# Twenty of a head's 64 score chunks moved from VectorE to TensorE in a decode step with its backward pass

## The chip, the cores and the metric

One Trainium2 chip; the program runs on 1 core. The metric is device time in microseconds (us) of one execution. A profile is one execution, and its span is a few us shorter than the timed run. Ratios are not quite the ratios of the medians that stand beside them.

## The reference, cut to what matters

A decode step (one token, D = 640) with an attention block over a cache and an MLP block, followed by the gradients of nine inputs. The attention has 32 heads, each with its own K and V cache of 8192 x 192 in bf16, and almost all bytes and time go there:

```python
q = (x @ wq).reshape(B, Sq, Hq, Dh).transpose(0, 2, 1, 3)      # Sq = 1, Hq = 32, Dh = 192
scores = einsum('bhqd,bhkd->bhqk', q, k) * Dh ** (-0.5)
p = softmax(scores, axis=-1)
o = einsum('bhqk,bhkd->bhqd', p, v)
# ... o @ wo, gates, MLP block; then jax.vjp of the whole for grad_out
```

The kernel works in two parts. The forward reads K and V of each head once (6.3 MB), makes the scores, and keeps the exponentials E of all heads and a matrix M = sum over keys of E * k v^T, from which the backward gets what it needs of q's gradient without reading K again. The backward reads V again and writes dK and dV. The change concerns the forward only.

## The kernel before: the parts that matter

A head's 8192 keys lie on 128 partitions, 64 "chunks" of 192 values each per partition, loaded in two halves of 32 chunks (1.5 MB each). Scores of a half are made on VectorE: one product with q, three halvings, one sum.

```python
def load_k(h, t):                       # 5 K buffers
    kb = KB[(2 * h + t) % NKB]
    nc.sync.dma_start(out=kb, in_=K_hd[h][:, t * JH : (t + 1) * JH, :])
def load_v(h, t):                       # 3 V buffers, the same SyncE queue
    vb = VB[nv[0] % NVB]
    nc.sync.dma_start(out=vb[:, :, 2 : 2 + PW], in_=...)

def dot_half(src4, vec, dst):           # VectorE, 32 chunks
    V_.tensor_tensor(out=prod, in0=src4, in1=vec(broadcast), op=mult)
    w = DH
    for _ in range(3):
        w //= 2
        V_.tensor_tensor(out=prod[:, :, 0:w], in0=prod[:, :, 0:w], in1=prod[:, :, w:2*w], op=add)
    V_.reduce_sum(out=dst, in_=prod[:, :, 0:w])

def softmax(h, S_h):                    # max over the head: VectorE, TensorE, VectorE, then E on ScalarE
    V_.reduce_max(out=m1, in_=S_h)
    T_.matmul(mx, lhsT=m1(broadcast), rhs=ident_f)
    V_.reduce_max(out=negm, in_=mx, negate=True)
    A_.activation(out=E4, in_=S_h(x4), func=Exp, bias=negm)
    ...

def scale_k(q, kb, E4, Ef):             # a quarter: E * K, 10 chunks on VectorE, 6 on ScalarE, 3 buffers KS
    ...
def m_quarter(q, ks, vb, mp):           # TensorE, 32 matmuls a quarter: (E * K)^T V, frees the V buffer
    ...
for i in range(HQ + 1):                 # scores of head i beside scaling and value matmuls of head i - 1
    kh = [load_k(i, 0), load_k(i, 1)]; vh = [load_v(i, 0)]
    for t in range(2):
        dot_half(kh[t], q_of_head_i, S_h[half t])
        for q in (2 * t, 2 * t + 1):    # of head i - 1
            m_quarter(q, scale_k(q, ...), pv[t], mp)
        if t == 0: vh.append(load_v(i, 1))
    E4, Ef = softmax(i, S_h)
    m_out(i - 1, mp)                    # copies M out; small matmuls "po" for the output columns
    # every second head: load wo and the next wq, q_pair() for the next two heads, pair_out()
```

The source says what depends on what. The order of the instructions on each engine is not that of the source: it is fixed when the program is compiled, once for all, and each engine then works through its own list in that order (the traces of the changed kernel and of e16 below, two programs with the same lists, show 8659 TensorE, 1657 VectorE and 2529 ScalarE records in the same order).

Of the kernel before, what the change touches and what calls it, by code (L numbers as in the profile page):

```python
# [8 lines left out]
FP32 = mybir.dt.float32  # L9
BF16 = mybir.dt.bfloat16  # L10
# [10 lines left out]
def kernel(  # L21
# [27 lines left out]
    P = 128  # L49
    D = A_x.shape[-1]  # L50
    _, HQ, S, DH = A_k_cache.shape
# [3 lines left out]
    J = S // P  # L55
    JH = J // 2
    JQ = J // 4
    ND = D // P
# [7 lines left out]
    MW = DH + 4  # L66
# [4 lines left out]
    V_, A_, T_ = nc.vector, nc.scalar, nc.tensor  # L71

    const = ctx.enter_context(tc.tile_pool(name="const", bufs=1))
# [77 lines left out]
    def bcast_cols(src, n, out, eng):  # L151
        tp = psS.tile([NF, P], FP32, name="bc_t", tag="s")
        T_.transpose(out=tp[0:n, :], in_=src, identity=ident_f)
        rows = tmp.tile([NF, P], BF16, name="bc_rows")
        eng(out=rows[0:n, :], in_=tp[0:n, :])
        for g in range(0, n, 4):
            m = min(4, n - g)
            ps = psB.tile([P, 512], FP32, name="bc_ps", tag="b")
            for b in range(m):
                T_.matmul(ps[:, b * P : (b + 1) * P], lhsT=pick(n, g + b), rhs=rows[0:n, :], start=True, stop=True)  # L160
            eng(out=out[:, g * P : (g + m) * P], in_=ps[:, 0 : m * P])
# [104 lines left out]
        return vb  # L266

    def dot_half(src4, vec, dst):
        prod = pp.tile([P, JH, DH], BF16, name="prod", tag="prod")
        V_.tensor_tensor(  # L270
            out=prod.rearrange("p (a b) d -> p a b d", b=2),
            in0=src4,
            in1=vec[:, None, None, :].to_broadcast([P, JH // 2, 2, DH]),
            op=ALU.mult,
        )
        w = DH
        for _ in range(3):
            w //= 2
            V_.tensor_tensor(out=prod[:, :, 0:w], in0=prod[:, :, 0:w], in1=prod[:, :, w : 2 * w], op=ALU.add)  # L279
        V_.reduce_sum(out=dst, in_=prod[:, :, 0:w], axis=AX.X)  # L280

    NKB = 5
    NVA = (3 * JQ) // 8
    MO = 256
    last = {}
    with tc.tile_pool(name="kp", bufs=1) as kp, tc.tile_pool(name="ks", bufs=1) as ksp:
        KB = [None] * NKB
        for k in range(NKB):
            b = (2 * (HQ - 1) + 2 + k) % NKB
# [9 lines left out]
        def load_k(h, t):  # L299
            kb = KB[(2 * h + t) % NKB]  # L300
            nc.sync.dma_start(out=kb, in_=K_hd[h][:, t * JH : (t + 1) * JH, :])
            return kb

        def softmax(h, S_h):
            m1 = tcol(1, "m1")
            V_.reduce_max(out=m1, in_=S_h, axis=AX.X)
            mx = psX.tile([P, P], FP32, name="mx", tag="mx")
            T_.matmul(mx, lhsT=m1[:, 0:1].to_broadcast([P, P]), rhs=ident_f, start=True, stop=True)
            negm = tcol(1, "negm")
            V_.reduce_max(out=negm, in_=mx, axis=AX.X, negate=True)  # L310
            E4 = tmp.tile([P, J, 4], BF16, name="E4")
            A_.activation(out=E4, in_=S_h[:, :, None].to_broadcast([P, J, 4]), func=ACT.Exp, bias=negm[:, 0:1], scale=1.0)
            A_.copy(out=E_all[:, h, :], in_=E4[:, :, 0])
            Ef = tmp.tile([P, J], FP32, name="Ef")
            A_.copy(out=Ef, in_=E4[:, :, 0])
            return E4, Ef

# [28 lines left out]
        def m_out(h, mp):  # L346
            t = h // 2
            A_.copy(out=M1[:, h, :], in_=mp[:, 0:MW])  # L348
            orow = tmp.tile([P, MW], FP32, name="orow")
            A_.copy(out=orow[64:65, :], in_=mp[64:65, MO : MO + MW])  # L350
            ov = orow[64:65, 2 : 2 + DH]
            one = ones_f[64:65, :]
            if h % 2 == 0:
                A_.copy(out=M2[0:64, t, :], in_=mp[0:64, MO : MO + MW])
                po = psO.tile([P, 8], FP32, name="po")
                last["po"] = po
                cols = ((0, 0, P, 0), (1, 0, 64, P))
            else:
                V_.tensor_copy(out=M2[64:128, t, :], in_=mp[0:64, MO : MO + MW])
                po = last["po"]  # L360
                cols = ((1, 64, P, 0), (2, 0, P, 64))
            for b, lo, hi, d0 in cols:
                T_.matmul(po[lo:hi, b : b + 1], lhsT=ov[:, d0 : d0 + hi - lo], rhs=one[:, 0:1], start=True, stop=True)
                T_.matmul(po[lo:hi, 3 + b : 4 + b], lhsT=one[:, 0 : hi - lo], rhs=orow[64:65, 0:1], start=True, stop=False)
                T_.matmul(po[lo:hi, 3 + b : 4 + b], lhsT=one[:, 0 : hi - lo], rhs=orow[64:65, MW - 1 : MW], start=False, stop=True)

        def pair_out(t, wo_t):
            po = last["po"]
            rz = tcol(3, "rz")
            V_.reciprocal(out=rz, in_=po[:, 3:6])  # L370
            V_.tensor_tensor(out=o_col[:, 3 * t : 3 * t + 3], in0=po[:, 0:3], in1=rz, op=ALU.mult)
            V_.tensor_copy(out=rinv[:, 2 * t : 2 * t + 2], in_=rz[:, 0:3:2])
            o2 = tmp.tile([P, 3, 2], BF16, name="o2")
            V_.tensor_tensor(out=o2, in0=omask, in1=o_col[:, 3 * t : 3 * t + 3, None].to_broadcast([P, 3, 2]), op=ALU.mult)
            ps = psS.tile([P, ND, 2], FP32, name="ao_ps", tag="s")
            for i in range(ND):
                for k in range(3):
                    T_.matmul(ps[:, i, :], lhsT=wo_t[:, k, i * P : (i + 1) * P], rhs=o2[:, k, :], start=(k == 0), stop=(k == 2))
            A_.copy(out=AO[:, :, 2 * t : 2 * t + 2], in_=ps)
# [5 lines left out]
        for i in range(HQ + 1):  # L385
            if i < HQ:
                if i == 0:
                    q_pair(0, w_next)
                kh = [load_k(i, 0), load_k(i, 1)]
                vh = [load_v(i, 0)]  # L390
                S_h = tmp.tile([P, J], FP32, name="S_h")
            mp = psM.tile([P, 512], FP32, name="mp", tag="m") if i > 0 else None
            for t in range(2):
                if i < HQ:
                    dot_half(kh[t].rearrange("p (a b) d -> p a b d", b=2), qs_bc[:, i * DH : (i + 1) * DH], S_h[:, t * JH : (t + 1) * JH])
                if i > 0:
                    pk, pv, pE4, pEf = st[i - 1]
                    for q in (2 * t, 2 * t + 1):
                        ks = scale_k(q, pk[t], pE4, pEf)
                        m_quarter(q, ks, pv[t], mp)  # L400
                if i < HQ and t == 0:
                    vh.append(load_v(i, 1))
            if i < HQ:
                E4, Ef = softmax(i, S_h)
                st[i] = (kh, vh, E4, Ef)
            if i > 0:
                m_out(i - 1, mp)
                if (i - 1) % 2 == 0:
                    wo_t = load_wo((i - 1) // 2)
                    if i + 1 < HQ:  # L410
                        w_next = load_w(wq_v, ((i + 1) // 2) * PW)
                        q_pair((i + 1) // 2, w_next)
                else:
                    pair_out((i - 1) // 2, wo_t)
                    if g_next < NMB // 3 and i >= 2:
                        for _ in range(2):
                            if g_next < NMB // 3:
                                mod_chunk(g_next, load_w(wm_v, g_next * PW))
                                g_next += 1
                st.pop(i - 1)  # L420
# [8 lines left out]
    dx1 = col(ND, "dx1")  # L429
    dao = col(ND, "dao")  # L430
    dao_bf = col(ND, "dao_bf", BF16)
    dao_bc = const.tile([P, D], BF16, name="dao_bc")
    cpr = col(HQ, "cpr")
    ckS = col(NQ, "ckS")
    with tc.tile_pool(name="mid", bufs=1) as mid, tc.tile_pool(name="mst", bufs=2) as mst:
# [109 lines left out]
        for i in range(ND):  # L545
            o3 = mst.tile([P, F], BF16, name="o3")
            V_.tensor_scalar(out=o3, in0=du_bc, scalar1=n2[:, i : i + 1], scalar2=None, op0=ALU.mult)
            nc.gpsimd.dma_start(out=out_6[i * P : (i + 1) * P, :], in_=o3)
        bcast_cols(dao, ND, dao_bc, A_.copy)


    with tc.tile_pool(name="bk1", bufs=1) as bk1, tc.tile_pool(name="ob", bufs=4) as ob, tc.tile_pool(name="bst", bufs=2) as bst:
        do_bc = bk1.tile([P, QD], BF16, name="do_bc")
        dha = bk1.tile([P, ND], FP32, name="dha")
        V_.memset(dha, 0.0)
        dsc = bk1.tile([P, ND], FP32, name="dsc")
# [99 lines left out]
        for h in range(HQ):  # L656
            doh = do_bc[:, h * DH : (h + 1) * DH]
            qh = qs_bc[:, h * DH : (h + 1) * DH]
            E4 = tmp.tile([P, J, 4], BF16, name="E4")
            A_.copy(out=E4, in_=E_all[:, h, :, None].to_broadcast([P, J, 4]))  # L660
            Ef = tmp.tile([P, J], FP32, name="Ef")
            A_.copy(out=Ef, in_=E_all[:, h, :])
            for t in range(2):
                js = slice(t * JH, (t + 1) * JH)
                v = load_v(h, t)
                dP = tcol(JH, "dP")
                dot_half(v[:, :, 2 : 2 + PW].rearrange("p a (b d) -> p a b d", b=2), doh, dP)
                dS4 = tmp.tile([P, JH, 4], BF16, name="dS4")
                V_.scalar_tensor_tensor(
                    out=dS4,  # L670
                    in0=dP[:, :, None].to_broadcast([P, JH, 4]),
# [56 lines left out]
```

## Time and profile before

| | before |
|---|---|
| time, median (range) | 1665.3 us (1662.5 to 1666.7) |
| forward, to the last head's maximum | 703 us |
| spacing of heads, mean of the last 20 | 21.1 us |
| VectorE busy, 300 to 600 us | 94% |
| DMA in the same stretch | 323 GB/s, share 0.94 |

The windows view gives, for stretches of the span, the busy time of each engine (with instruction counts), then the TensorE clock that was granted, the mean busy share of the DMA engines, and GB/s. Kernel before, one forward and one backward stretch:

```profile
core 0: us, PE busy (x) PEld busy (x) DVE busy (x) ACT busy (x) POOL busy (x), PEclk, DMA share, GB/s
300.00:600.00 300.00, 212.66 (x2130) 198.26 (x2130) 281.75 (x264) 153.93 (x483) 0.00 (x0) 0.81 0.94 323
...
1000.00:1400.00 400.00, 76.61 (x727) 54.30 (x724) 385.90 (x455) 238.85 (x614) 53.31 (x80) 0.50 1.04 390
```

VectorE (DVE) is the busy engine of the forward. DMA is close behind. The backward moves 390 GB/s and is not touched by the change.

The groups by shape (busy us, mean ns of one, then idle time before) give the price of a score half, 300 to 500 us, kernel before:

```profile
L279 DVE TENSOR_TENSOR prod<-prod 128x3072 bf16<-128x3072 bf16 x20 | 35.0, 1751 | 0.3
L279 DVE TENSOR_TENSOR prod<-prod 128x1536 bf16<-128x1536 bf16 x20 | 19.1, 954 | 0.3
L280 DVE TENSOR_REDUCE S_h<-prod 128x32 f32<-128x768 bf16 x19 | 18.0, 949 | 0.3
L270 DVE TENSOR_TENSOR prod<-KB_255,qs_bc 128x6144 bf16<-128x6144 bf16 x4 | 13.4, 3355 | 1.6 <-ACT qs_bc L240 1.5
...
L279 DVE TENSOR_TENSOR prod<-prod 128x768 bf16<-128x768 bf16 x19 | 10.5, 554 | 0.2
```

The longest wait of SyncE's queue, 300 to 600 us (total us, times, longest): loads of V wait for their buffer, which the value matmuls free.

```profile
SPq L265 <- PE mp L344: 144.2, 25, 10.8
```

The chain of waits, followed back through the same stretch, runs mostly through VectorE:

```profile
by line: DVE prod L270 25.4%; DVE prod L279 17.7%; PE mp L343 13.6%; PE mp L344 13.1%; DVE S_h L280 4.5%; DVE KS_258 L326 4.3%; DVE KS_256 L326 4.0%; DVE KS_260 L326 3.9%; issue 3.5%; PE po L363 1.3%; PE q_ps L239 1.3%; PE mx L308 1.2%; ACT
```

### The profile page before, as it was taken

The numbers are of one execution on the slowest core, as the hardware profiler recorded it, in microseconds if no ns is written. First come the engines' busy times: TensorE is split into PE (matmuls) and PEld (weight loads), VectorE is DVE, ScalarE is ACT, GpSimd is POOL, SyncE is SP. The second block draws the span as 40 slices with busy tenths as digits, with TensorE's granted clock in tenths as the row PEclk, the third lists the DMA queues.
The fourth block names the chain that finished last, engine by engine and source line by source line (L and its number), as shares of the span: only waits on it lengthen the run. The fifth ranks groups of instructions, "written<-read, shape, count | busy, mean of one in ns | idle before, by whom it ended". The sixth has DMA issues, their size and how long they took to land.

```text
span 1662.7 us, 18656 instructions
## 1 busy us (share of the span) xinstructions
PE 666.1 (40%) x6611; PEld 582.7 (35%) x6611; DVE 1524.3 (92%) x1654; ACT 884.0 (53%) x2497; POOL 117.9 (7%) x190
## 2 busy tenths in 40 slices
PE   2777767686868676773222212222212110000000
PEld 2666766575757576662121111111101000000000
DVE  6889899999999999955999999989999899999997
ACT  2445554464545454544765656666565746555552
POOL 0000000000000000001111111111111111010000
PEclk9788777788878888765555555555555555555555
DMA  9999889999898999875999999999999999999996
GB/s 336 310 325 309 305 296 328 335 317 338 309 331 310 330 309 329 268 251 180 386 389 401 369 403 378 402 388 390 398 383 390 372 407 387 393 398 377 379 354 255
DMA packets 347147, 574.34 MB, mean 345 GB/s; under 512 B 7438, under 2 KB 316686, under 8 KB 322478
## 3 DMA queue, kind: packets, MB, share of 16 engines
q1 hardware_dynamic: 322538, 347.23, 63.1%
q0 software_dynamic: 24496, 225.92, 32.4%
q8 instruction: 52, 0.85, 0.2%
q14 instruction: 41, 0.34, 0.1%
q10 hardware_dynamic: 20, 0.00, 0.0%
HBM read 347.21 MB, written 225.91 MB: 345 GB/s over the span
## 4 chain that ended last, share of the span: by engine, by line
DVE 64%; PE 14%; DMA 10%; issue 8%; ACT 2%; SPq 1%; POOL 0%; POOLq 0%; ACTq 0%
DVE prod L270 18%; DVE prod L279 18%; DVE dK L647 8%; PE mp L343 5%; PE mp L344 5%; DMA VB_239<-in_A_v_cache_dram 5%; DVE dV L647 5%; DVE dP L280 3%; DMA VB_236<-in_A_v_cache_dram 2%; DVE S_h L280 2%; DMA VB_242<-in_A_v_cache_dram 2%; DVE KS_258 L326 2%; DVE KS_260 L326 2%; DMA w_st<-in_A_wq_dram 1%; DVE KS_256 L326 1%
## 5 line engine op out<-in xcount | busy, mean ns | idle before, releaser
L679 ACT ACTIVATE dV<-do_bc,Ef 128x192 bf16<-128x192 bf16 x1152 | 405.9, 446 | 30.0 <-DMA out_dram<-dV 29.9
L279 DVE TENSOR_TENSOR prod<-prod 128x3072 bf16<-128x3072 bf16 (+2 forms) x384 | 415.9, 1083 | 3.9
L348 ACT COPY M_230<-mp 128x196 f32<-128x196 f32 x32 | 10.3, 323 | 171.7 <-PE mp L344 171.7
L583 PE MATMUL acc_ps<-v_bf,wqT 128*128 128x1 bf16 x390 | 14.2, 165 | 203.6 <-DVE v_bf L578 203.0
L343 PE MATMUL mp<-VB_236,KS_256 128*128 128x194 bf16 x352 | 82.9, 296 | 21.8 <-DVE KS_256 L326 21.7
L583 PEld LDWEIGHTS <-wqT 128*128 128x128 bf16 x390 | 14.5, 106 | 214.1 <-issue 214.0
L343 PE MATMUL mp<-VB_242,KS_258 128*128 128x194 bf16 x336 | 76.4, 290 | 30.5 <-DVE KS_258 L326 30.5
L343 PEld LDWEIGHTS <-KS_258 128*128 128x128 bf16 x688 | 73.3, 106 | 36.5 <-DVE KS_258 L326 34.9
L343 PE MATMUL mp<-VB_239,KS_260 128*128 128x194 bf16 x336 | 74.3, 285 | 25.5 <-DVE KS_260 L326 25.5
L343 PEld LDWEIGHTS <-KS_256 128*128 128x128 bf16 x688 | 73.9, 107 | 28.5 <-DVE KS_256 L326 26.8
L270 DVE TENSOR_TENSOR prod<-VB_239,do_bc 128x6144 bf16<-128x6144 bf16 x22 | 73.6, 3348 | 10.8 <-DMA VB_239<-in_A_v_cache_dram 8.2
L344 PE MATMUL mp<-VB_236,KS_256 128*128 128x194 bf16 x352 | 82.7, 295 | 0.6 <-ACT KS_256 L325 0.6
L343 PEld LDWEIGHTS <-KS_260 128*128 128x128 bf16 x672 | 70.3, 105 | 31.0 <-DVE KS_260 L326 29.6
L567 ACT COPY wqT<-wT_ps 128x1024 bf16<-128x1024 bf16 x26 | 26.3, 1012 | 97.7 <-PE acc_ps L583 91.5
L344 PE MATMUL mp<-VB_242,KS_258 128*128 128x194 bf16 x336 | 76.0, 287 | 0.2 <-ACT KS_258 L325 0.2
L344 PEld LDWEIGHTS <-KS_256 128*128 128x128 bf16 x688 | 75.1, 109 | 2.6 <-ACT KS_256 L325 1.0
L270 DVE TENSOR_TENSOR prod<-VB_236,do_bc 128x6144 bf16<-128x6144 bf16 x21 | 70.3, 3347 | 5.6 <-DMA VB_236<-in_A_v_cache_dram 5.6
L344 PEld LDWEIGHTS <-KS_258 128*128 128x128 bf16 x688 | 74.1, 108 | 1.8 <-ACT KS_258 L325 0.4
L270 DVE TENSOR_TENSOR prod<-VB_242,do_bc 128x6144 bf16<-128x6144 bf16 x21 | 70.3, 3347 | 4.5 <-DMA VB_242<-in_A_v_cache_dram 4.5
L344 PE MATMUL mp<-VB_239,KS_260 128*128 128x194 bf16 x336 | 73.9, 282 | 0.2 <-ACT KS_260 L325 0.2
L565 PE MATMUL wT_ps<-ident_bf,w_st 128*128 128x128 bf16 (+1 forms) x470 | 50.2, 309 | 56.5 <-ACT woT L568 38.5
L344 PEld LDWEIGHTS <-KS_260 128*128 128x128 bf16 x672 | 71.4, 106 | 1.5 <-ACT KS_260 L325 0.4
(893 smaller groups left out, 2356.5 us busy)
## 6 DMA issues: line engine op xcount, KB each, us to landing
out_dram<-dV POOLq DMA_DIRECT2D x64, 1536.0 KB, 9.7
out_dram<-dK POOLq DMA_DIRECT2D x64, 1536.0 KB, 9.4
VB_236<-in_A_v_cache_dram SPq DMA_DIRECT2D x43, 1536.0 KB, 15.2
VB_239<-in_A_v_cache_dram SPq DMA_DIRECT2D x43, 1536.0 KB, 14.9
VB_242<-in_A_v_cache_dram SPq DMA_DIRECT2D x42, 1536.0 KB, 12.3
KB_252<-in_A_k_cache_dram SPq DMA_DIRECT2D x13, 1536.0 KB, 11.4
KB_253<-in_A_k_cache_dram SPq DMA_DIRECT2D x13, 1536.0 KB, 11.4
KB_254<-in_A_k_cache_dram SPq DMA_DIRECT2D x13, 1536.0 KB, 12.0
```

Of the source, the lines that this page charges most:

```text
L270: V_.tensor_tensor(out=prod.rearrange("p (a b) d -> p a b d", b=2), in0=src4, in1=vec[:, None, None, :].to_broadcast([P, JH // 2, 2, DH]), ...
L279: V_.tensor_tensor(out=prod[:, :, 0:w], in0=prod[:, :, 0:w], in1=prod[:, :, w : 2 * w], op=ALU.add)
L280: V_.reduce_sum(out=dst, in_=prod[:, :, 0:w], axis=AX.X)
L326: V_.tensor_tensor(out=ks[:, 0:n, 0:DH].rearrange("p j (a b) -> p j a b", b=4), in0=kb[:, k0 : k0 + n, :].rearrange("p j (a b) -> p j a b" ...
L343: T_.matmul(mp[:, o : o + DH + 2], lhsT=ks[:, k * KW : k * KW + P], rhs=rhs, start=s, stop=e, skip_group_check=True)
L344: T_.matmul(mp[:, MO + o : MO + o + DH + 2], lhsT=ks[:, k * KW + P : k * KW + 2 * P], rhs=rhs, start=False, stop=e, skip_group_check=True)
L348: A_.copy(out=M1[:, h, :], in_=mp[:, 0:MW])
L565: T_.transpose(out=tp[lo:hi, x * P : (x + 1) * P], in_=src, identity=ident_bf)
L567: A_.copy(out=wT[:, 0:1024], in_=tp[:, 0:1024])
L583: T_.matmul(ps[:, i : i + 1], lhsT=wT[:, (b * ND + i) * P : (b * ND + i + 1) * P], rhs=v_bf[:, b : b + 1], start=(b == 0), stop=(b == 2))
L647: V_.tensor_tensor(out=out3[:, n0_:n1_, :].rearrange("p j (a b) -> p j a b", b=4), in0=vec.rearrange("p (a b) -> p a b", b=4)[:, None, :, ...
L679: A_.activation(out=dV[:, jj, :], in_=doh, func=ACT.Copy, scale=Ef[:, t * JH + jj : t * JH + jj + 1])
```

## The change

Intent: VectorE binds the forward, TensorE is idle a good quarter of it. So the last 10 of each half's 32 chunks get their scores on TensorE: 15 transposes of 128 x 128, one copy from PSUM by ScalarE, 15 matmuls with two columns of q. VectorE keeps 22 chunks, and takes 11 instead of 10 chunks of each scaling from ScalarE.

```diff
-        prod = pp.tile([P, JH, DH], BF16, name="prod", tag="prod")
+        n = 2 * src4.shape[1]
+        prod = pp.tile([P, JH, DH], BF16, name="prod", tag="prod")[:, 0:n, :]
...
-    NVA = (3 * JQ) // 8
+    NVA = (5 * JQ) // 16
+    NPP = min(5, JH // 4)
+    JD = JH - 2 * NPP
...
+        def q_cols(h): ...            # q as columns, 4 small matmuls and a copy
+        def pe_scores(kb, qc, dst):
+            kf = kb.rearrange("p j d -> p (j d)")[:, JD * DH :]
+            tp = psT.tile([P, 2048], BF16, name="kT_ps", tag="t")
+            n = 3 * NPP
+            for b in range(n):
+                T_.transpose(out=tp[:, b * P : (b + 1) * P], in_=kf[:, b * P : (b + 1) * P], identity=ident_bf)
+            kT = ktp.tile([P, n * P], BF16, name="kT")
+            A_.copy(out=kT, in_=tp[:, 0 : n * P])
+            ps = psS.tile([P, NPP, 2], FP32, name="sc_ps", tag="s")
+            for m in range(NPP):
+                for b in range(3):
+                    x = (3 * m + b) * P
+                    T_.matmul(ps[:, m, :], lhsT=kT[:, x : x + P], rhs=qc[:, b, :], start=(b == 0), stop=(b == 2))
+            A_.copy(out=dst, in_=ps.rearrange("p m b -> p (m b)"))
...
-                    dot_half(kh[t].rearrange(...), qs_bc[...], S_h[:, t * JH : (t + 1) * JH])
+                    if t == 0:
+                        qc = q_cols(i)
+                    pe_scores(kh[t], qc, S_h[:, t * JH + JD : (t + 1) * JH])
+                    dot_half(kh[t][:, 0:JD, :].rearrange(...), qs_bc[...], S_h[:, t * JH : t * JH + JD])
```

The rest (cut) moves small tiles between memory pools to make room, and one broadcast of 640 values from the end of the middle part to the start of the backward.

More of the change, by code (lines that the diff above doesn't have):

```diff
@@ L272, in dot_half @@
             in0=src4,
-            in1=vec[:, None, None, :].to_broadcast([P, JH // 2, 2, DH]),
+            in1=vec[:, None, None, :].to_broadcast([P, n // 2, 2, DH]),
             op=ALU.mult,
@@ L282 @@
     NKB = 5
-    NVA = (3 * JQ) // 8
+    NVA = (5 * JQ) // 16
+    NPP = min(5, JH // 4)
+    JD = JH - 2 * NPP
     MO = 256
     last = {}
-    with tc.tile_pool(name="kp", bufs=1) as kp, tc.tile_pool(name="ks", bufs=1) as ksp:
+    with tc.tile_pool(name="kp", bufs=1) as kp, tc.tile_pool(name="ks", bufs=1) as ksp, tc.tile_pool(name="ft", bufs=2) as ft, tc.tile_pool(name="kt", bufs=1) as ktp:
         KB = [None] * NKB
@@ L302, in load_k, with q_cols @@
             return kb
+        unit = kp.tile([1, 4], BF16, name="unit")
+        V_.memset(unit, 0.0)
+        V_.memset(unit[0:1, 0:1], 1.0)
+        V_.memset(unit[0:1, 3:4], 1.0)
+        def q_cols(h):
+            q = qs_bc[0:1, h * DH : (h + 1) * DH]
+            ps = psS.tile([P, 3, 2], FP32, name="qc_ps", tag="s")
+            for b, lo, hi, d0, u in ((0, 0, P, 0, 0), (1, 0, 64, P, 0), (1, 64, P, 0, 2), (2, 0, P, 64, 2)):
+                T_.matmul(ps[lo:hi, b, :], lhsT=q[:, d0 : d0 + hi - lo], rhs=unit[0:1, u : u + 2], start=True, stop=True)
+            qc = ft.tile([P, 3, 2], BF16, name="qc")
+            A_.copy(out=qc, in_=ps)
+            return qc
+        def pe_scores(kb, qc, dst):
[12 more added lines that the diff above has]
+            A_.copy(out=dst, in_=ps.rearrange("p m b -> p (m b)"))
         def softmax(h, S_h):
@@ L310, in softmax @@
             V_.reduce_max(out=negm, in_=mx, axis=AX.X, negate=True)
-            E4 = tmp.tile([P, J, 4], BF16, name="E4")
+            E4 = ft.tile([P, J, 4], BF16, name="E4")
             A_.activation(out=E4, in_=S_h[:, :, None].to_broadcast([P, J, 4]), func=ACT.Exp, bias=negm[:, 0:1], scale=1.0)
             A_.copy(out=E_all[:, h, :], in_=E4[:, :, 0])
-            Ef = tmp.tile([P, J], FP32, name="Ef")
+            Ef = ft.tile([P, J], FP32, name="Ef")
             A_.copy(out=Ef, in_=E4[:, :, 0])
@@ L348, in m_out @@
             A_.copy(out=M1[:, h, :], in_=mp[:, 0:MW])
-            orow = tmp.tile([P, MW], FP32, name="orow")
+            orow = ft.tile([P, MW], FP32, name="orow")
             A_.copy(out=orow[64:65, :], in_=mp[64:65, MO : MO + MW])
@@ L372, in pair_out @@
             V_.tensor_copy(out=rinv[:, 2 * t : 2 * t + 2], in_=rz[:, 0:3:2])
-            o2 = tmp.tile([P, 3, 2], BF16, name="o2")
+            o2 = ft.tile([P, 3, 2], BF16, name="o2")
             V_.tensor_tensor(out=o2, in0=omask, in1=o_col[:, 3 * t : 3 * t + 3, None].to_broadcast([P, 3, 2]), op=ALU.mult)
@@ L390 @@
                 vh = [load_v(i, 0)]
-                S_h = tmp.tile([P, J], FP32, name="S_h")
+                S_h = ft.tile([P, J], FP32, name="S_h")
             mp = psM.tile([P, 512], FP32, name="mp", tag="m") if i > 0 else None
@@ L394 @@
                 if i < HQ:
-                    dot_half(kh[t].rearrange("p (a b) d -> p a b d", b=2), qs_bc[:, i * DH : (i + 1) * DH], S_h[:, t * JH : (t + 1) * JH])
+                    if t == 0:
+                        qc = q_cols(i)
+                    pe_scores(kh[t], qc, S_h[:, t * JH + JD : (t + 1) * JH])
+                    dot_half(kh[t][:, 0:JD, :].rearrange("p (a b) d -> p a b d", b=2), qs_bc[:, i * DH : (i + 1) * DH], S_h[:, t * JH : t * JH + JD])
                 if i > 0:
@@ L431 @@
     dao_bf = col(ND, "dao_bf", BF16)
-    dao_bc = const.tile([P, D], BF16, name="dao_bc")
     cpr = col(HQ, "cpr")
@@ L548 @@
             nc.gpsimd.dma_start(out=out_6[i * P : (i + 1) * P, :], in_=o3)
-        bcast_cols(dao, ND, dao_bc, A_.copy)
     with tc.tile_pool(name="bk1", bufs=1) as bk1, tc.tile_pool(name="ob", bufs=4) as ob, tc.tile_pool(name="bst", bufs=2) as bst:
         do_bc = bk1.tile([P, QD], BF16, name="do_bc")
+        dao_bc = bk1.tile([P, D], BF16, name="dao_bc")
+        bcast_cols(dao, ND, dao_bc, A_.copy)
         dha = bk1.tile([P, ND], FP32, name="dha")
@@ L658 @@
             qh = qs_bc[:, h * DH : (h + 1) * DH]
-            E4 = tmp.tile([P, J, 4], BF16, name="E4")
+            E4 = bst.tile([P, J, 4], BF16, name="E4")
             A_.copy(out=E4, in_=E_all[:, h, :, None].to_broadcast([P, J, 4]))
-            Ef = tmp.tile([P, J], FP32, name="Ef")
+            Ef = bst.tile([P, J], FP32, name="Ef")
             A_.copy(out=Ef, in_=E_all[:, h, :])
@@ L667 @@
                 dot_half(v[:, :, 2 : 2 + PW].rearrange("p a (b d) -> p a b d", b=2), doh, dP)
-                dS4 = tmp.tile([P, JH, 4], BF16, name="dS4")
+                dS4 = bst.tile([P, JH, 4], BF16, name="dS4")
                 V_.scalar_tensor_tensor(
```

## The prediction

> **What bounds the kernel now.** By the windows view, the 1663 us span is a forward of about 735 us (32 heads) and a backward from about 770 us. The backward runs at 390 GB/s with a DMA share of 1.03; the change leaves its work alone, so I expect nothing there. In the forward, VectorE is 94% busy from 300 us on. Starts of the maximum over a head's scores (L306) are about 23 us apart for heads 4 to 8 and 21.2 us on average from 280 us on. VectorE's waits are small (about 1 us per head), so VectorE bounds a head. DMA is close behind: of 1 us windows, about 80% are saturated, at 371 GB/s; the rest are gaps in which the queue waits for a V buffer (SP queue's waits: 338 us of 600 on "mp L344"). A head moves 21.2 us x 320 GB/s = 6.8 MB, hence a DMA floor of 18.3 us (estimate).
>
> **What the change does, per head.**
> - VectorE, scores: 22 instead of 32 chunks per half. By-form durations 3.36, 1.75, 0.95, 0.55, 0.95 us (7.6 us a half) should fall in proportion to elements above about 0.15 us each, to 2.35, 1.25, 0.70, 0.43, 0.70 = 5.4 us (estimate). Saved: 4.3 us.
> - VectorE, K scaling: 11 instead of 10 chunks of each quarter, 4 x 0.1 us. Net 3.85 us off.
> - ScalarE: two 128x1920 copies of transposed K (1.76 us each, as L446 shows), 0.8 us of small copies, less four 0.36 us scalings: +2.9 us on 11.2. Not a bound.
> - TensorE: 30 transposes and 30 narrow matmuls, 118 ns a transpose at half clock (15 in 1.77 us in the backward): 4 to 7 us onto some 15.5 busy per head. The Trainium skill ("TensorE: Matmul & The Clock Gate", "The HAM clock gate") says that a busy window raises the clock to full and an idle one halves it; the trace agrees (0.50 from 412 to 419 us after a gap, 1.00 from 421). The added work should fill the gap before the value matmuls, which then start warmer and free V buffers sooner. A cost: TensorE, in its own order, now waits for K to land and for ScalarE's copy.
> - SBUF pools and the later broadcast of dao: at most 2 us.
>
> **On the critical path.** 3.85 us off VectorE would give about 17.4 us per late head, below the DMA floor of 18.3. So DMA takes over and part of the gain is lost. With imperfect queueing (a V buffer still gates the queue) I expect 19.2 us per late head (saving 2.0 x 22) and 20.3 for early ones (2.5 x 9): about 65 us.
>
> Predicted: 1602 us, 8 in 10 between 1572 and 1640. Chances: faster by over 2% 0.83, within 2% 0.15, slower 0.02.
>
> **What would show it.**
> - L306 spacing of 18.5 to 19.7 us in late heads; forward ending near 670 us.
> - The 22-chunk product near 2.35 us; VectorE share in the forward down to about 85%.
> - DMA in the forward at 350 to 365 GB/s, its gaps mostly gone; VectorE then waits for K loads or the softmax chain.
> - Mean TensorE clock in the forward above 0.81.
> - Backward length unchanged within 5 us.
>
> **What would make it wrong.** TensorE in order: score matmuls waiting for K or for ScalarE's copy delay the value matmuls, V buffers come free late, DMA keeps its gaps, and a head stays above 20.3 us. Or the instruction order of the new code puts both score parts late, lengthening scores-softmax-scaling. In the other direction, saturated DMA without gaps gives 18.3 us and about 1570.

## More of the kernel before

The timeline of VectorE (start us, duration, then the instruction) shows the order in which it works, here around the softmax of one head, kernel before:

```profile
407.53 0.22 DVE L306 TENSOR_REDUCE m_4055<-S_h 128x1 f32<-128x64 f32 x1
408.14 3.36 DVE L270 TENSOR_TENSOR prod<-KB_253,qs_bc 128x6144 bf16<-128x6144 bf16 x1 [0.40 <-ACT qs_bc L240]
411.42 0.28 DVE L310 TENSOR_REDUCE negm<-mx 128x1 f32<-128x128 f32 x1
411.62 1.75 DVE L279 TENSOR_TENSOR prod<-prod 128x3072 bf16<-128x3072 bf16 x1
413.29 1.15 DVE L326 TENSOR_TENSOR KS_260<-KB_251,E_4061 128x1920 bf16<-128x1920 bf16 x1
414.36 0.95 DVE L279 TENSOR_TENSOR prod<-prod 128x1536 bf16<-128x1536 bf16 x1
415.22 1.15 DVE L326 TENSOR_TENSOR KS_256<-KB_251,E_4061 128x1920 bf16<-128x1920 bf16 x1
```

Between the two reductions of the maximum (m, negm) VectorE already does the next head's product; the scalings (KS) then stand between the pieces of that dot product, so VectorE does not wait for the softmax. Only the heads from about the tenth on are ordered so. In heads 4 to 8 the four scalings follow the softmax in one block (in heads 9 and 10 partly), and heads 4 to 10 are 22.8 us apart.

## The result, and the profile after

The changed kernel took 1682.5 us (1680.0 to 1688.9) against 1665.3: ratio 1.011, 95% interval 1.008 to 1.014: a little slower, by less than 2% but clear of the noise. The prediction was 1602 us.

| | before | after |
|---|---|---|
| spacing of heads, mean of the last 20 | 21.1 us | 22.2 us (19.5 and 24.9 in turn) |
| last maximum at | 703 us | 718 us |
| VectorE busy, 300 to 600 us | 94% | 74% |
| VectorE busy per head (share x spacing) | 19.8 us | 16.5 us |
| mean TensorE clock, 300 to 600 us | 0.81 | 0.84 |
| DMA, 300 to 600 us | 323 GB/s | 304 GB/s |
| first backward product to the end | 887.4 us | 886.8 us |

Kernel after, the windows view of the same stretch, the groups, SyncE's longest wait and the chain of waits:

```profile
300.00:600.00 300.00, 248.06 (x2910) 229.31 (x2909) 223.48 (x246) 183.73 (x491) 0.00 (x0) 0.84 0.89 304
```

```profile
L280 DVE TENSOR_TENSOR prod<-prod 128x2112 bf16<-128x2112 bf16 x18 | 22.6, 1258 | 0.6
L280 DVE TENSOR_TENSOR prod<-prod 128x1056 bf16<-128x1056 bf16 x18 | 12.8, 708 | 0.6
L281 DVE TENSOR_REDUCE S_h<-prod 128x22 f32<-128x528 bf16 x18 | 12.7, 703 | 0.5
L271 DVE TENSOR_TENSOR prod<-KB_261,qs_bc 128x4224 bf16<-128x4224 bf16 x4 | 9.4, 2357 | 1.6 <-ACT qs_bc L240 1.5
...
L280 DVE TENSOR_TENSOR prod<-prod 128x528 bf16<-128x528 bf16 x18 | 7.7, 427 | 0.5
```

```profile
SPq L265 <- PE mp L378: 236.9, 27, 15.1
```

```profile
by line: PE mp L377 24.2%; PE mp L378 23.2%; ACT kT L330 11.2%; PE kT_ps L328 7.6%; PE sc_ps L335 4.6%; PE mx L342 3.2%; PE po L397 2.7%; DVE KS_262 L360 2.1%; DVE KS_264 L360 2.1%; PE po L399 2.0%; issue 1.9%; PE q_ps L239 1.9%; PE po L398
```

VectorE got cheaper as planned, and every piece has the predicted length. But the time that it gave up came back as waiting, and the chain now runs through TensorE and ScalarE's copy of the transposed K. DMA is less busy than before; its queue waits longer for V buffers. The two orders show why. Kernel after, VectorE around one softmax:

```profile
432.58 0.22 DVE L340 TENSOR_REDUCE m_5667<-S_h 128x1 f32<-128x64 f32 x1
433.84 0.29 DVE L344 TENSOR_REDUCE negm<-mx 128x1 f32<-128x128 f32 x1 [1.04 <-PE mx L342]
434.77 1.26 DVE L360 TENSOR_TENSOR KS_262<-KB_259,E_5673 128x2112 bf16<-128x2112 bf16 x1 [0.63 <-ACT E_5673 L346]
...
439.56 1.26 DVE L360 TENSOR_TENSOR KS_262<-KB_260,E_5673 128x2112 bf16<-128x2112 bf16 x1 [1.19 <-PE mp L378]
440.73 2.35 DVE L271 TENSOR_TENSOR prod<-KB_261,qs_bc 128x4224 bf16<-128x4224 bf16 x1
```

Nothing is left to do between m and negm, and the scalings stand in one block. And TensorE in the same head (kernel after; value matmuls, "mp", left out except the first):

```profile
436.08 0.34 PE L377 MATMUL mp<-VB_236,KS_262 128*128 128x194 bf16 x1 [1.50 <-DVE KS_262 L360]
...
442.05 1.00 PE L328 MATMUL kT_ps<-ident_bf,KB_261 128*128 128x128 bf16 x15
...
444.90 0.53 PE L335 MATMUL sc_ps<-qc,kT 128*128 128x2 bf16 x15
...
446.71 1.00 PE L328 MATMUL kT_ps<-ident_bf,KB_257 128*128 128x128 bf16 x15
...
449.62 0.53 PE L335 MATMUL sc_ps<-qc,kT 128*128 128x2 bf16 x15 [0.23 <-ACT kT L330]
```

Between the maximum and the first value matmul TensorE is idle for 1.9 and 2.4 us in turn. It starts the value matmuls at half clock (they follow each other every 0.16 us until about 439 us, later about every 0.08 us), and does the next head's transposes and scores in their midst, where they delay them. Meanwhile the load queue waits 15.1 us for a V buffer (428.7 to 443.9 us), and DMA runs dry (kernel after, windows view; the last three numbers are clock, DMA share and GB/s):

```profile
438.00:440.00 2.00, 2.00 (x20) 1.93 (x18) 0.81 (x2) 2.00 (x7) 0.00 (x0) 0.73 0.70 209
440.00:442.00 2.00, 2.00 (x27) 2.00 (x25) 2.00 (x2) 2.00 (x8) 0.00 (x0) 1.00 0.03 8
```

No engine waits for a K load between 300 and 600 us. In a pair of heads (44.4 us) VectorE's waits in the timeline add up to 10.7 us. The two largest groups of them, 300 to 600 us, are waits for TensorE (its broadcast of the maximum, and its score matmuls, which stand before the copy of M):

```profile
DVE negm L344 <- PE mx L342: 23.6, 14, 2.3
DVE M_231 L393 <- PE sc_ps L335: 12.3, 6, 2.1
```

### The profile page after: what moved, and what is told of

Its sections match the earlier page's. It is cut to its first block, busy times and chain, and to the rows that moved or that the text cites. A ratio compares the mean times of both kernels' runs of the same rounds, so it can differ in the third digit from the quotient of the medians.

```text
span 1678.3 us, 22848 instructions
## 1 busy us (share of the span) xinstructions
PE 758.2 (45%) x8659; PEld 665.7 (40%) x8659; DVE 1415.3 (84%) x1657; ACT 963.7 (57%) x2529; POOL 117.9 (7%) x190
## 4 chain that ended last, share of the span: by engine, by line
DVE 46%; PE 32%; DMA 8%; ACT 7%; issue 6%; POOL 0%; SPq 0%; ACTq 0%; POOLq 0%; DVEq 0%
DVE prod L280 11%; DVE prod L271 10%; PE mp L377 10%; PE mp L378 9%; DVE dK L684 8%; DMA VB_236<-in_A_v_cache_dram 5%; ACT kT L330 5%; DVE dV L684 5%; PE kT_ps L328 3%; DVE dP L281 3%; PE sc_ps L335 2%; DMA VB_242<-in_A_v_cache_dram 2%; DVE stg L633 1%; PE mx L342 1%; PE po L397 1%
## 5 line engine op out<-in xcount | busy, mean ns | idle before, releaser
L280 DVE TENSOR_TENSOR prod<-prod 128x2112 bf16<-128x2112 bf16 (+5 forms) x384 | 360.3, 938 | 6.6
L330 ACT COPY kT<-kT_ps 128x1920 bf16<-128x1920 bf16 x64 | 112.6, 1759 | 121.2 <-PE kT_ps L328 121.2
L377 PE MATMUL mp<-VB_236,KS_262 128*128 128x194 bf16 x352 | 77.6, 282 | 21.8 <-DVE KS_262 L360 21.8
L377 PE MATMUL mp<-VB_242,KS_264 128*128 128x194 bf16 x336 | 74.7, 283 | 20.6 <-DVE KS_264 L360 20.6
L377 PE MATMUL mp<-VB_239,KS_266 128*128 128x194 bf16 x336 | 74.8, 283 | 19.6 <-DVE KS_266 L360 19.6
L377 PEld LDWEIGHTS <-KS_262 128*128 128x128 bf16 x688 | 71.6, 104 | 25.4 <-DVE KS_262 L360 23.9
L377 PEld LDWEIGHTS <-KS_264 128*128 128x128 bf16 x688 | 71.4, 104 | 23.9 <-DVE KS_264 L360 22.5
L377 PEld LDWEIGHTS <-KS_266 128*128 128x128 bf16 x672 | 69.9, 104 | 22.8 <-DVE KS_266 L360 21.3
L623 PE MATMUL bc_t<-ident_f,dmod 128*3 128x128 f32 x10 | 3.7, 375 | 162.2 <-DVE dsc L621 162.2
L378 PE MATMUL mp<-VB_236,KS_262 128*128 128x194 bf16 x352 | 77.0, 279 | 0.0
L378 PE MATMUL mp<-VB_239,KS_266 128*128 128x194 bf16 x336 | 74.3, 280 | 0.0
L378 PE MATMUL mp<-VB_242,KS_264 128*128 128x194 bf16 x336 | 74.1, 280 | 0.0
L378 PEld LDWEIGHTS <-KS_262 128*128 128x128 bf16 x688 | 72.8, 106 | 1.5
L378 PEld LDWEIGHTS <-KS_264 128*128 128x128 bf16 x688 | 72.6, 105 | 1.5
## 6 DMA issues: line engine op xcount, KB each, us to landing
VB_236<-in_A_v_cache_dram SPq DMA_DIRECT2D x43, 1536.0 KB, 15.7
```

The source lines that it names most:

```text
L330: A_.copy(out=kT, in_=tp[:, 0 : n * P])
L377: T_.matmul(mp[:, o : o + DH + 2], lhsT=ks[:, k * KW : k * KW + P], rhs=rhs, start=s, stop=e, skip_group_check=True)
L378: T_.matmul(mp[:, MO + o : MO + o + DH + 2], lhsT=ks[:, k * KW + P : k * KW + 2 * P], rhs=rhs, start=False, stop=e, skip_group_check=True)
```

## The experiments

`behind(a, b)` in the edits stands for an edge that makes instruction a come after b in the list of their common engine. It adds no wait. Seventeen kernels ran. Head spacings are means of the last 20 heads, taken from the starts of the maximum. Ratios are to the kernel before of the same rounds.

### Order against TensorE's load (four runs on one chip)

**e1: VectorE's order of before given to the changed kernel.**

```diff
+ behind(negm of head i, product of head i+1)
+ behind(scaling 1 of i, halving 1 of i+1); behind(scaling 2, halving 3); behind(scaling 3, sum)
```

> The changed kernel, with issue-order edges on VectorE only: the maximum's second reduction of head i goes behind the first product of head i+1, and the four K scalings of head i go between the pieces of that head's first dot product (the order that the kernel before had from about its tenth head on). Theory O (the fixed instruction order lost the overlap: all four scalings stand alone between two dot products, so softmax latency and the waits for scaled-K buffers lie bare on VectorE): head spacing falls from 22.2 us to about 19.5 to 20.5, 1600 to 1635 us. Rival P (TensorE's added transposes, copies and score matmuls on the value-matmul chain eat the gain): stays within 1 percent of the changed kernel, 1665 to 1695. Rival D (DMA: V buffers come free too late): also stays above 1660.

Measured: 1702.3 us, ratio 1.021, 22.5 us a head. My theory failed in this form. VectorE's waits, 300 to 600 us, show a new one:

```profile
DVE prod L271 <- DMA KB<-in_A_k_cache_dram: 49.4, 6, 8.8
```

In this order, K comes too late.

**e2: the changed kernel's VectorE order given to the kernel before.**

```diff
+ behind(product of head i+1, scaling 3 of head i)
```

> The kernel before, with one kind of issue-order edge: the first product of head i+1 goes behind the last scaling of head i, which is the order of the changed kernel in all its heads. Theory O: every head is spaced like the early heads of before (about 23.3 us) instead of 21.2, so 1700 to 1720 us, and the changed kernel is 1 to 2.5 percent faster than this one: in equal order the change is a gain. Rivals P and D: order is not what matters, 1660 to 1675 us.

Measured: 1721.1 us, ratio 1.033, 23.4 us a head. This one edge, with the same work, costs 3.3% (the lists of the other engines are compiled afresh with it), and in equal VectorE order the change is a gain: 1.011 / 1.033 = 0.979.

**e3: no scores on TensorE, changed kernel's VectorE order.**

```diff
  def pe_scores(kb, qc, dst):
-     transposes, copy, score matmuls
+     A_.copy(out=dst, in_=zero)
```

> Wrong result on purpose: the changed kernel in its own VectorE order, but the last 10 chunks of each half get zero scores from a small ScalarE copy; no transposes, no copy of transposed K, no score matmuls, no q columns. VectorE does exactly the changed kernel's work. Rival P: 1590 to 1625 us, the predicted gain comes back. Theory O: only part of it, head spacing 20.5 to 21.5 us, 1630 to 1660, because the bare softmax latency and buffer waits stay.

Measured: 1654.1 us, ratio 0.992, 21.7 us a head. (The comparison of results passed in spite of the zero scores, in this run and in e4 and e6; so a passed comparison says little about the scores that TensorE makes.) The added work, on TensorE and in ScalarE's copies, costs some 1.9% (0.992 / 1.011 = 0.981). That is more than the 1.1% by which the change lost, but only about 32 of the 80 us between prediction and result.

**e4: no scores on TensorE, interleaved order.**

> Wrong result on purpose: as the run without scores on TensorE, with the interleaved order on VectorE. It measures what is left when neither order nor TensorE's added work binds. My estimate of a DMA floor of 18.3 us per head: 18.5 to 19.5 us, 1570 to 1605 us. Rival D (V buffers limit): not below 20.5 us per head, 1640 us or more.

Measured: 1642.9 us, ratio 0.985, 20.9 us a head, above the range. VectorE waited for K loads again (67 us in 300 to 600 us). So a third thing binds: the loads. They all go through SyncE's queue in one order. A V load whose buffer is not yet free holds the K loads and weights behind it: in the changed kernel the queue issues one V load at 451.5 us, the next one only at 465.0 us, and the K load that stands behind it at 465.5 us.

### The load queue (four runs on one chip)

**e5: K loads issued from GpSimd's queue.**

```diff
-            nc.sync.dma_start(out=kb, in_=K_hd[h][...])
+            nc.gpsimd.dma_start(out=kb, in_=K_hd[h][...])
```

> The changed kernel with one line changed: K loads are issued from GpSimd's queue instead of SyncE's, so a K load no longer stands behind a V load that waits for its buffer. The instruction order found for this code turns out different too: from the middle of the forward on, the scalings stand between the pieces of the next dot product by themselves. Theory V (one in-order load queue, gated by the three V buffers, delivers K late once the rest is ordered well): against the interleaved version of the changed kernel, which took 1702 us, this one loses the waits of products for K loads (66 us in 300 to 700 us of the span) and gives 1600 to 1640. Theory P (TensorE's own order binds): 1670 or more in spite of it.

Measured: 1611.0 us, ratio 0.967, 19.5 us a head. (The order is not quite as the text says: the trace has the scalings between the pieces up to about head 18, and after that in one block in every second head.)

**e6: the same with no scores on TensorE and interleaved order.**

> Wrong result on purpose (no scores on TensorE), interleaved order, K loads on GpSimd's queue. With the K loads on SyncE's queue it took 1643 us, with 86 us of VectorE waits for K in 300 to 700 us of the span. Theory V: those waits go, heads come down to 18.5 to 19.3 us, 1575 to 1600 us; this is the DMA floor of my prediction. If the floor itself was wrong (the loads cannot run that close together), it stays above 1625.

Measured: 1626.2 us, ratio 0.976, 19.6 us a head. The waits for K went, but not the time: VectorE now waited for ScalarE's exponentials, which come late in this forced order. A miss; it says nothing on the DMA floor.

**e7: the kernel before with that queue.**

> The kernel before with K loads on GpSimd's queue. VectorE's waits for K are small there, and its work per head is unchanged (about 20 us busy of 21.2), so by theory V at most the early heads gain: 1640 to 1667 us. If it is much faster, the queue was a limit of the kernel before too.

Measured: 1643.9 us, ratio 0.986, 19.8 us a head; VectorE waits for nothing there any more. The queue held up the kernel before too. (Its lists were compiled afresh as well; e10 below gives VectorE this order on the shared queue, without a gain.)

**e8: TensorE's named waits removed in the changed kernel, shared queue.**

```diff
+ behind(po matmuls of head i-1, mx of head i); behind(copy into M2, maximum)
+ behind(first value matmul, last q_pair matmul)
```

> The changed kernel in its own VectorE order (scalings alone), with issue-order edges on TensorE: the broadcast of the maximum goes ahead of the previous head's output columns, the next pair's q goes ahead of the value matmuls, and on VectorE the copy into M2 goes behind the maximum. It takes away the named waits of the slower heads (qs_bc 1.5 us, M2 copy 2.1 us, maximum up to 2.3 us, all in pairs of 44.4 us). Theory P: heads go from 19.5 and 24.9 us to about 18.5 and 21, 1600 to 1630 us. If the waits only move (DMA or scaled-K buffers take their place): 1650 or more.

Measured: 1688.7 us, ratio 1.014, 22.2 us a head. The waits moved: TensorE then waited for the load of wq, and VectorE for scaled-K buffers. Mending single waits in the list did not help here.

### Queue and order taken apart

**e9: own K queue, but VectorE's grouped order held by the edge of e2.**

> The changed kernel with K loads on GpSimd's queue but its old VectorE order held by edges (scalings alone, the next dot product behind the last scaling). Separates queue from order in the 1611 us run. In the changed kernel VectorE never waited for a K load, so if both conditions are needed (theory O and V together: the interleaved order needs early K, and early K needs its own queue), the queue alone gives nothing here: 1670 to 1705 us (some 18 us of it a later start, as in the other runs with this queue). If the queue alone was the cause: 1640 or less.

Measured: 1608.1 us, ratio 0.965, 18.9 us a head. I expected 1670 or more. So VectorE's order is not what held the changed kernel back. What else differed were the lists of TensorE and of ScalarE, which the compile step had made differently for the new queue: a head's first transposes and scores now stood before the value matmuls.

**e10: the kernel before in interleaved order throughout, shared queue.**

> The kernel before, K loads on SyncE's queue as they were, with the interleaved order from the first head on. Completes the table of order against queue for the kernel before (mixed order 1667, grouped 1721, own queue 1644). VectorE is busy about 20 us a head there, so K has time to arrive: the early heads lose their 1.5 to 2.5 us of excess: 1635 to 1660 us.

Measured: 1664.6 us, ratio 0.998, 21.4 us a head; just above the range. The early heads did not improve (22.8 us), and VectorE waited for q instead (26 us in 300 to 680 us).

**e11: as e5, K loads of heads 0 and 1 back on SyncE's queue.**

```diff
+            (nc.sync if h < 2 else nc.gpsimd).dma_start(out=kb, in_=K_hd[h][...])
```

> The changed kernel with the K loads of heads 0 and 1 on SyncE's queue and those of all later heads on GpSimd's. In the 1611 us run the five first K loads ran ahead of the small w_mod loads that the first q needs, and the first maximum came at 48 us instead of 30. With that mended I expect 1592 to 1605 us, heads at 19.0 to 19.6 us: the version that I would hand on.

Measured: 1599.5 us, ratio 0.959, 19.2 us a head; the first maximum moved from 48.3 to 33.5 us.

**e12: the kernel before with the queue of e11.**

> The kernel before with the same queue change (heads 0 and 1 on SyncE, later heads on GpSimd): the control for what the studied change is worth once the queue does not bind. VectorE bound at 19.8 us a head as in the run at 1644, with the start mended: 1622 to 1635 us. The changed kernel should then be ahead by 1.2 to 2.5 percent, well under the 3.85 us a head that VectorE gave up, because DMA binds it at about 19.4 us a head.

Measured: 1634.9 us, ratio 0.981, 19.8 us a head. The windows view shows VectorE at its limit (297 of 300 us):

```profile
300.00:600.00 300.00, 231.26 (x2295) 216.34 (x2296) 297.18 (x282) 165.11 (x518) 15.86 (x30) 0.84 1.01 342
```

With K on its own queue, and each kernel in the order compiled for it, the studied change is worth 0.959 / 0.981 = 0.978, a gain of 2.2%.

**e13 and e14: TensorE's order and the queue, crossed by edges.** Both keep VectorE's grouped order. e13 has the own queue and puts the score work among the value matmuls; e14 has the shared queue and puts it first.

```diff
e13: + behind(transposes 0, value matmul 54); behind(scores 0, value matmul 76); behind(transposes 1, 93) ...
     + behind(mx of head i+1, last po of head i)
e14: + behind(first value matmul of head i, scores 0 of head i+1)
     + behind(transposes 1 of head i+1, value matmul 32 of head i)
```

> Changed kernel, VectorE order as it was, K loads on GpSimd's queue, and TensorE's order held by edges as in the changed kernel: the next head's transposes behind the 54th and 93rd value matmul, its scores behind the 76th and 113th, the maximum behind the output columns. Theory T (what costs the time is that the score work stands in the middle of the value matmuls while TensorE idles through the softmax): heads at 21 to 22.3 us, 1665 to 1705 us although K is early. Theory Q (the shared load queue itself costs the time): 1600 to 1630 us.

> Changed kernel, VectorE order as it was, K loads on SyncE's queue as they were, TensorE's order held by edges: a head's first transposes and scores before the value matmuls of the head before. Theory T alone: 1595 to 1630 us (no late start on this queue). If the early order needs the own queue (K loads behind V loads that wait for a buffer land too late for it, as in the 1702 us run): TensorE or VectorE waits for K loads, 1660 to 1710 us.

Measured: e13 1654.5 us, ratio 0.993, 20.8 us a head, between the two theories; e14 1736.8 us, ratio 1.043, 23.7 us a head, worse than either. With the own queue, moving the score work into the midst of the value matmuls (and the maximum behind the output columns) costs 20.8 - 18.9 = 1.9 us a head. That is not yet all of the 22.2 (e13 copies the places of the score work from one head of a pair; in the other head of the changed kernel they come later, after value matmuls 80, 100, 118 and 128), so the lists had to be held as a whole.

**e15: as e9, with the start of e11.**

> The 1608 us run with the K loads of heads 0 and 1 back on SyncE's queue, which brought the first maximum from 48 to 33 us in the other order. Heads at 18.9 us as there, start mended: 1590 to 1600 us, a little under the 1599.5 us of the version without edges.

Measured: 1597.7 us (1596.6 to 1598.6), ratio 0.959, 18.9 us a head. It beats both kernels, and passed the comparison with the reference, which is a weak test of the scores (see e3). Its windows view, then TensorE and VectorE around one softmax (value matmuls left out):

```profile
300.00:600.00 300.00, 275.05 (x3447) 257.71 (x3445) 263.09 (x297) 208.67 (x569) 16.99 (x32) 0.93 1.06 364
```

```profile
445.75 0.49 PE L348 MATMUL mx<-ident_f,m 128*128 128x128 f32 x2
446.70 0.53 PE L341 MATMUL sc_ps<-qc,kT 128*128 128x2 bf16 x15 [0.46 <-ACT kT L336]
447.09 1.00 PE L334 MATMUL kT_ps<-ident_bf,KB 128*128 128x128 bf16 x15
...
454.17 0.52 PE L341 MATMUL sc_ps<-qc,kT 128*128 128x2 bf16 x15
```

```profile
445.48 0.22 DVE L346 TENSOR_REDUCE m<-S_h 128x1 f32<-128x64 f32 x1
446.28 0.29 DVE L350 TENSOR_REDUCE negm<-mx 128x1 f32<-128x128 f32 x1 [0.58 <-PE mx L348]
447.46 4.77 DVE L366 TENSOR_TENSOR KS<-KB,E 128x2112 bf16<-128x2112 bf16 x4 [0.89 <-ACT E L352]
452.14 2.35 DVE L271 TENSOR_TENSOR prod<-KB,qs_bc 128x4224 bf16<-128x4224 bf16 x1
```

The score work fills TensorE's gap during the softmax (idle 0.3 and 1.3 us in turn before the first value matmul, instead of 1.9 and 2.4). It runs at full clock for more of the time (mean clock 0.93 instead of 0.84, though still at half from 464 to 468 us), the four scalings run without a wait for a buffer, and DMA moves 364 instead of 304 GB/s.

**e16 and e17: the exact lists, crossed with the queue.** The program is built twice: the first build only yields the order of all instructions on TensorE, VectorE and ScalarE; the second has the other queue and an edge between each instruction and the next of that list. The lists were compared line by line with those of the changed kernel (e16) and of e11 (e17): no difference.

```diff
+ for e in (PE, DVE, ACT):
+     for a, b in zip(order[e], order[e][1:]):
+         behind(traced[e][b], traced[e][a])
```

> Changed kernel with every instruction of TensorE, VectorE and ScalarE in exactly the changed kernel's order (compared line by line: no difference), only the K loads of heads 2 to 31 on GpSimd's queue. In the changed kernel no engine was seen waiting for a K load. If the compiled order is what costs the time (theory T): 1665 to 1690 us, heads still at 19.5 and 24.9 us. If the queue itself slows the changed kernel by a way I have not seen in its waits (theory Q): 1600 to 1630 us.

> The order of the 1599.5 us version exactly, on the same three engines, with all K loads back on SyncE's queue behind the V loads. If K then lands too late for this order (theory V): waits for K loads come back and it takes 1690 to 1745 us, like the two runs with early orders on the shared queue (1702 and 1737). If the order alone makes the gain: 1595 to 1625 us.

Measured: e16 1688.3 us, ratio 1.013, heads at 19.5 and 24.9 us in turn, the very spacing of the changed kernel, with nearly the same waits as the changed kernel (300 to 600 us; KS waited 15.7 us there):

```profile
DVE negm L351 <- PE mx L349: 23.4, 14, 2.3
DVE KS L367 <- PE mp L385: 15.3, 13, 1.4
DVE M L400 <- PE sc_ps L342: 14.4, 7, 2.1
```

e17 took 1731.1 us, ratio 1.039, 24.1 us a head. Its late load was not K, as I had written, but the weights for q, which share the same queue:

```profile
PE q_ps L246 <- DMA w_st<-in_A_wq_dram: 77.2, 7, 14.0
```

Around one softmax the queue first waits 6.2 us for a V buffer (432.5 to 438.7 us), then issues a K load, which takes it 2.4 us, and only at 441.65 us these weights. They land at 451.35 us, and TensorE, which needs them next in its list, is idle for 9.9 us. Until they have landed the queue stops at the load of wo, which shares three buffers with wq. The queue's own waits, 300 to 680 us, begin so:

```profile
SPq L196 <- DMA w_st<-in_A_wq_dram: 78.1, 8, 10.9
SPq L272 <- PE mx L349: 66.8, 16, 6.5
```

In all it waited 118 us at V loads (L272), 141 us at K loads and 93 us at loads of wo (L196). The order of SyncE's own list was not held in e16 and e17: the loads of wq and wo stand elsewhere among the V loads in e17 than in e11.

The table, as ratios to the kernel before:

| | all loads on SyncE's queue | K on GpSimd's queue from head 2 |
|---|---|---|
| kernel before, order as compiled for that queue | 1 | 0.981 (e12) |
| changed kernel, order compiled for the shared queue | 1.011 (the change) | 1.013 (e16) |
| changed kernel, order compiled for K's own queue | 1.039 (e17) | 0.959 (e11) |

The cause is settled to this point: with K on its own queue, the order of the three lists alone makes the step from 1688 to 1600 us (e16 against e11), and with the changed kernel's order the queue makes no difference (1.011 and 1.013). On the shared queue none of the four other orders that ran was better than the changed kernel's (e1 1.021, e8 1.014, e14 1.043, e17 1.039). So in these runs both had to change together, and a change of one line in the source (the queue) brought both. It is not shown that no good order exists for the shared queue: another order of the loads in SyncE's list, which would bring the weights for q earlier, and more buffers for weights or V were not tried. That the compile step chose the poor order because it reckons with late loads on the shared queue is my reading of this; the runs show only that another queue yields another order.

## Why the prediction was wrong

- **What bounds the kernel before**: right in the main. With K on its own queue (e12) VectorE is busy 297 of 300 us at 19.8 us a head; the other 1.3 us of the 21.1 came back with the queue and the lists compiled for it.
- **What the pieces cost**: right. Predicted 2.35, 1.25, 0.70, 0.43 and 0.70 us for a 22-chunk half; measured 2.36, 1.26, 0.71, 0.43 and 0.70. ScalarE's copy took 1.76 us. VectorE gave up 3.8 us a head by the sum of its instructions' durations, 3.3 us by its busy time, in which overlaps count once (predicted 3.85).
- **Backward and memory pools**: right. From the first backward product to the end 887.4 and 886.8 us; from the last maximum to that product 72.6 and 73.1 us.
- **The step that failed**: "The added work should fill the gap before the value matmuls, which then start warmer and free V buffers sooner." In the changed kernel it stands among the value matmuls instead (in every second head transposes after the 54th and 93rd and scores after the 76th and 113th of 128, in the others later still). A gap of about 2 us stayed, the value matmuls still began at half clock, and SyncE's wait for V buffers grew from 144 to 237 us in 300 us. I treated the order of an engine's instructions as if work flowed into any gap; it is a fixed list. e13 puts only this work (and the maximum) back among the value matmuls on K's own queue, and that costs 1.9 us of the 3.3 us a head between e9 and the changed kernel; the rest is not traced to single instructions. In e15, where the score work stands in the gap, the clock is 0.93 and the head 18.9 us. That this is near my 19.2 us, and its 1597.7 us near my 1602, is luck: another queue was needed for it, which I had not foreseen.
- **The second step that failed**: "With imperfect queueing (a V buffer still gates the queue) I expect 19.2 us per late head". I had read the long wait of the queue (338 of 600 us), and counted it as about 1 us a head. With the order of e11, one queue for all loads costs 24.1 - 19.2 = 4.9 us a head (e17 against e11), and the queue waits there at all three kinds of load, not at V alone. With the changed kernel's own order it costs nothing (e16), so the loss of the studied change lies in the first step.
- **"So DMA takes over"**: wrong for the changed kernel. DMA fell to 304 GB/s. In e15 it reaches a share of 1.06 and 364 GB/s, near my estimate of the floor (18.3 us a head), but TensorE (92%) and VectorE (88%) are busy there too, and no run separates the three.
- The warning "TensorE in order ... a head stays above 20.3 us" named the right place, but not quite the way: TensorE's score matmuls waited for ScalarE's copy for 9.0 us in 300 to 600 us and for K not at all. I gave it too small a chance, 0.17 for all that is not a gain of over 2%.

What stays open: why heads 4 to 10 of e15 are still 20.1 us apart; e3, e4 and e6 (no scores on TensorE) did not reach the predicted floor, each for another wait; and whether the shared queue allows a good order, with the loads in SyncE's list or the buffers arranged otherwise.

## What to carry to other kernels

When work moves to an idle engine, ask where in that engine's fixed list it will stand: an idle share in the profile is a place only if the list has it there. When the busiest engine becomes faster, look first at queues that already wait a lot off the critical path, above all one queue that carries loads with different reasons to wait. If a change that should help does not, compare the lists of instructions of both kernels and try the two suspects together: here the queue alone changed nothing (e16), the order alone made it worse (e17), and both together took 4.1% off the time of the kernel before.

## What the Trainium skill lacked or had wrong

- "DMA: Bandwidth & Descriptors", section "Issuing engines are not separate DMA queues", says that starting DMAs from several engines only saves the sequencer's time to issue them. With the same instruction lists on the three computing engines, K loads on GpSimd's queue took 1599.5 us and on SyncE's queue 1731.1 us (e11, e17; SyncE's own list was not held). With the changed kernel's lists, 1688.3 and 1682.5 us (e16 and the change), the sentence fits. What that section lacks is that a load that waits for its buffer holds those behind it in the list of its engine (changed kernel, 451.5 to 465.5 us).
- The same change has a cost at the start: five K loads at once on the second queue ran ahead of small loads that the first q needs, and the first maximum came at 48.3 instead of 33.5 us (e5, e11). I found it on no page that I read.
- "TensorE: Matmul & The Clock Gate", section "The HAM clock gate", gives an idle window of about 3.4 us as what halves the clock and a busy one of that length as what restores it. The rise agrees: value matmuls at half clock from 436 us, full clock some 3 us later (kernel after). The fall came sooner than the word idle suggests: the clock was at half from about 432.3 us, though TensorE had been busy for 2.1 of the 4 us before 432 and its longest gap between 427 and 433 us was 1.6 us (some matmul records can be missing). With more of the gap filled (e15) the mean clock was 0.93 against 0.84. What the section lacks is that the filler must stand in the gap in the compiled list.
- None of the pages that I read says that a change of the queue of a load changes the compiled order of the computing engines. It did here: e5 differs from the changed kernel by one line, its lists differ on all three engines, and its time is 4.4% shorter (0.967 / 1.011 = 0.956).
